# A w2 chunk loaded earlier, the fourfold copies and some ACT steps moved, and epsilon added on VectorE for two tiles

## The chip, the cores and the metric

One Trainium2 chip; the kernel runs on one of its cores. The metric is the device time of one execution in microseconds (us). Engines are called by their short names: PE is TensorE's matmul, PEld its weight load, DVE is VectorE, ACT is ScalarE, POOL is GpSimd, and SP is SyncE, which in this kernel issues nearly all DMA transfers.

## What is computed

The reference adds a residual, a linear attention and an MLP with squared ReLU, all on 2048 tokens of width 512:

```python
xn = _layernorm(x)                       # eps 1e-5
# A: 32 heads of 16
qkv = xn @ wqkv
phi = lambda t: where(t > 0, t + 1, exp(t)) + 1e-6
kv  = einsum("bhsd,bhse->bhde", phi(k), v)
z   = einsum("bhsd->bhd", phi(k))
o   = einsum("bhqd,bhde->bhqe", phi(q), kv) / (einsum("bhqd,bhd->bhq", phi(q), z) + 1e-6)
# B: F = 1376
h   = xn @ w1 + b1
h   = where(h > 0, h, 0) ** 2
return x + o @ wo + (h @ w2 + b2)
```

Inputs and output are float32. The kernel keeps that precision by splitting every operand into a high part in fp32r and the rest (a low part), and by running three matmuls (high by high, high by low, low by high) for each product.

## The kernel before, in words

The program is one long straight line for each engine: the order is written out by hand, and each engine runs its own instructions strictly in that order, waiting on semaphores. SP issues transfers in program order too, so a transfer that waits holds up those behind it.

**First part, tokens.** Sixteen tiles of 128 tokens are loaded, normalised (`measure` and `roots` for mean and root, `normalise`), transposed, projected onto k, and passed through phi. In `roots` (L239 to L243) POOL adds epsilon to the variance (L242) and raises it to the power -0.5 (L243); DVE then applies the result (L265). For each tile `kx` (L380 to L387) accumulates phi(k) against the tokens into four PSUM banks. Tokens carry a column of ones, so the last bank also holds the key sum z.

**Between the parts** (L864 to L985). The last `kx` is done, and ACT copies the four banks to `kxs` and one piece to `zrow` (L876). SP writes it to DRAM (`zd`, L878) and loads it back turned, in four transfers into `zc` (L882): these are the key sum's transfers. `zc` is first used well into the second part (L1125). PE forms the values and then, in `matrix`, four banks `pm`, which ACT copies (`matrix_copy`, tiles m); they are the attention matrix, needed split into mh and ml some 30 us later. The last chunk of w1 (96 of 128 columns, NF - 1 = 10) is applied ahead of the others as `pz` and `pz0b`, with ReLU into r2c. `piece_2(NF - 1, 0)` (L984) issues the loads of the last w2 chunk's rows (three transfers, L207, tile r2_10, shown as r) and returns two steps for later: `high` copies the rows on ACT into w2r (L210), sends part of that copy to another place of the same tile (L211) and, the first time only, makes the four copies w2q of 32 rows (L215); `low` has DVE compute the rest (L218, L219).

**Second part, two passes n = 0 and 1.** Each pass handles two blocks of 512 tokens, t1 and t2, with the transposed tokens x1 and x2. Pairs of weight chunks (two q chunks or two w1 chunks, `order`) are multiplied by both blocks with seven products instead of eight: sums S1 to S4 of weights (`chunk_sums`, split into `aop` by `chunk_split`) and sums T[1] to T[4] of tokens. Step p handles one pair; its PE order in step 0 of pass 0 is

- A by A11 with x1, then ACT copies bank A (c11, L1080);
- B by A12; then C by S1 with T[1], and ACT copies bank C (t5, L1097);
- `matrix` (pm, only here), then A by S2 with T[2], and ACT copies A (c12, L1162);
- C by S4 with x2, which needs the t5 copy to have read bank C;
- A by S3 with T[3], which needs the c12 copy to have read bank A;

and in step 1 the same again for the next pair, with the previous pair's last product (T[4], L1104, into the bank `before`) in between and, behind it, the first output product: `second_sums` (L1187) calls `last_2` (L493), eight matmuls on `acc` of the last w2 chunk with sz. sz is the squared r2c in fp32r, made by `last_units` (L960, ACT twice, then a transfer inside sz at L465 and DVE's rest in `rests`). Tiles T[3] and T[4] get their high parts on ACT and their low parts on DVE in `last_sums` (L1123, L1179); in the profile T_1014 is T[3] and T_1015 is T[4].

`next_2(t)` (L1002) carries out the two waiting steps of a w2 chunk (`high`, `low`) and issues the load of the next chunk. In the kernel before, `next_2(0)` stands at L1082, right behind the c11 copy of step 0. Raw weights of all kinds pass through one ring of six buffers (tag "raw"): a load waits until the last reader of the tile that held its buffer is done. `load_1` issues the two loads of a q or w1 pair (rq, r1) two steps ahead.

In the lines below a tile has no number, so r stands for r1, r2 and their like; the PSUM banks of the products are b, and c and t are the copies c11, c12 and t5.

Of the kernel before, what the change touches and what calls it, by code (L numbers as in the profile page):

```python
# [8 lines left out]
F32R = mybir.dt.float32r  # L9
AF = mybir.ActivationFunctionType  # L10
OP = mybir.AluOpType
# [7 lines left out]
def kernel(  # L19
# [30 lines left out]
    nc = tc.nc  # L50
# [9 lines left out]
    NF = -(-F // P)  # L60
# [11 lines left out]
    keep = ctx.enter_context(tc.tile_pool(name="keep", bufs=1))  # L72
# [5 lines left out]
    def bank(name, tag="ps"):  # L78
        return psum.tile([P, 512], F32, name=name, tag=tag)

    def w512(name, tag, bufs):
        return work.tile([P, 512], F32, name=name, tag=tag, bufs=bufs)
# [8 lines left out]
    def two(name):  # L91
        return keep.tile([P, 2, 512], F32, name=name, tag=next_tag("x"))

    def four(name, tag, dt=F32, pool=None):
        return (pool or work).tile([P, TB, 512], dt, name=name, tag=tag)
# [4 lines left out]
    def f32(ap):  # L100
        return ap.bitcast(F32)
# [7 lines left out]
    def copy(eng, o, i, bias=0.0):  # L109
        if eng == "act":  # L110
            nc.scalar.activation(o, i, AF.Copy, bias=bias)  # L111
        elif bias:
            ENG[eng].tensor_scalar(o, i, bias, None, op0=OP.add)
        else:
            ENG[eng].tensor_copy(o, i)
# [5 lines left out]
    def rest_of(l, src, h):  # L121
        nc.vector.tensor_tensor(out=l, in0=src, in1=f32(h), op=OP.subtract)  # L122
# [40 lines left out]
    def raw(name, src):  # L163
        t = w512(name, "raw", 6)
        nc.sync.dma_start(t[:, :src.shape[-1]], src)
        return t
# [6 lines left out]
    def units(f):  # L173


        if f < NF - 1:
            return [(0, f * P, P)]
        return [(0, f * P + Q, 2 * Q), (2 * Q, f * P, Q), (3 * Q, f * P, Q)]
# [5 lines left out]
            nc.sync.dma_start(tj[:, :, a:a + n], w1[:, o:o + n].rearrange("(j p) n -> p j n", j=NJ))  # L184
        return t

    w2r = []

    def load_o():
        o = wos[0] = four("wo", "ra")  # L190
# [6 lines left out]
    def piece_2(f, at):  # L197

        h, l = w2s[f] = [w2r[at // 2][:, at % 2 * 2 + u] for u in range(2)]
        if f < NF - 1:  # L200
            t = raw(f"r2_{f}", w2[f * P:(f + 1) * P, :])
            return [lambda: copy("act", h, t), lambda: rest_of(l, t, h)]


        t = w512(f"r2_{f}", "raw", 6)
        for a, o, n in units(f):
            nc.sync.dma_start(t[a:a + n], w2[o:o + n, :])  # L207

        def high():
            copy("act", h, t)  # L210
            nc.sync.dma_start(f32(l[2 * Q:]), f32(h[:2 * Q]))  # L211
            if "q" not in w2s:
                w2s["q"] = work.tile([P, D], F32R, name="w2q", tag="w2q")
                for k in range(TB):
                    nc.sync.dma_start(f32(w2s["q"][k * Q:(k + 1) * Q]), f32(h[2 * Q:3 * Q]))  # L215

        def low():
            rest_of(l[:2 * Q], t[:2 * Q], h[:2 * Q])  # L218
            rest_of(h[3 * Q:], t[3 * Q:], h[3 * Q:])  # L219

        return [high, low]
# [17 lines left out]
    def roots(tiles, st, mv, y):  # L239

        n = len(tiles)
        nc.gpsimd.tensor_scalar(y[:, 1, :n], mv[:, :n, 1], 1e-5, None, op0=OP.add)  # L242
        nc.gpsimd.tensor_tensor(out=y[:, 0, :n], in0=y[:, 1, :n], in1=power[:, :n], op=OP.pow)  # L243

    def normalise(tiles, st, mv, y):
# [206 lines left out]
    def quarters(name, r, h, pool, tag):  # L452

        lq = pool.tile([P, P], F32R, name=f"{name}q", tag=tag)
        for k in range(TB):
            at, to = slice(2 * Q, 3 * Q), slice(k * P, (k + 1) * P)
            rest_of(lq[k * Q:(k + 1) * Q], r[at, to], h[at, to])
        return lq

    def hidden_last(name, r):  # L460

        s = pair(name)
        h, hl = s[:, 0], s[:, 1]
        copy("act", h, r)
        nc.sync.dma_start(f32(hl[:2 * Q]), f32(h[:2 * Q]))  # L465

        def rests():
            rest_of(hl[2 * Q:], r[:2 * Q], h[:2 * Q])

        return (h, hl), rests  # L470

    def relu(o, i, f):
        nc.scalar.activation(o, i, AF.Relu, bias=b1s[:, f:f + 1])

    def plain_1(ps, w, x):

        for j in range(NJ):
            three(ps, [w[:, u, j * P:(j + 1) * P] for u in range(2)],
                  [x[u][:, j, :] for u in range(2)], j == 0, j == NJ - 1)
# [63 lines left out]
    for i0 in range(0, NT, TB):  # L543
# [5 lines left out]
        n = TB if i0 >= NPE else TB // 2  # L549
# [105 lines left out]
    def tokens_sum(n, tag):  # L655
        return keep.tile([P, 2, 2, 512], F32R, name=f"T{n}", tag=tag)
# [51 lines left out]
    def load_1(kind, n):  # L708
        load = raw_1 if kind == "w" else raw_q
        return [load(2 * n + k).rearrange("p (c n) -> p c n", c=2) for k in range(2)]  # L710
# [25 lines left out]
    def do(what, k=1):  # L736
        for _ in range(k):
            if what:
                what.pop(0)()
# [41 lines left out]
    def more(i=None):  # L781

        if i is None or i > 12:
            do(extra, counts[0].pop(0))
# [77 lines left out]
        more(i)  # L862

    T.update({n: tokens_sum(n, f"A{n - 3}") for n in (3, 4)})  # L864
    xlast = [xsb[(b + 1) % 2] for b in (NB - 1, NB - 2)]
    more()
    pz = bank("pz0")
# [47 lines left out]
    def matrix_copy(j, ps):  # L915
        if j % 2 == 0:
            mraw.append(two(f"m{j}"))
        copy("act", mraw[j // 2][:, j % 2], ps[j])
# [5 lines left out]


    last = TB - 1
    w2r = [four(f"w2r{k}", f"C{k}", F32R, keep) for k in range(2)]
    for n in range(2):
        t1, t2 = NB - 1 - 2 * n, NB - 2 - 2 * n
        x1, x2 = xsb  # L930
# [29 lines left out]
        def last_units(rz):  # L960
            nc.scalar.activation(rz, rz, AF.Square)
            sz, rests = hidden_last(f"sz{n}", rz)

            def packed():
                lqs.append(quarters(f"sz{n}", rz, sz[0], work, "heads"))

            return sz, rests, packed
# [3 lines left out]
        if n == 0:  # L971

            more()
            pz2 = bank("pz0b")
            plain_1(pz2, z, x2)
            more()

            rz = r2[1]
            relu(rz, pz, NF - 1)
            relu(r2[NF - 1], pz2, NF - 1)  # L980
            do(extra, 2)
            values()
            do(extra, len(extra))
            w2next = piece_2(NF - 1, 0)  # L984
        else:  # L985
            w2next = []
            pz = bank(f"pz{n}", "acc")
            plain_1(pz, z, x1)
# [4 lines left out]
        if n:  # L993
            rz = w512(f"rz{n}", "p", 6)
            relu(rz, pz, NF - 1)
            sz, sz_rests, packed = last_units(rz)
# [5 lines left out]
        def next_2(t):  # L1002

            do(w2next, 2 - highs.pop(0))
            if t + 1 < NF and (n == 0 or t >= TB - 1):
                f = w2order[t + 1]
                w2next.extend(piece_2(f, place(f)))
# [40 lines left out]
        def step(k=1):  # L1048

            for _ in range(k):  # L1050
                do(steps[t1] or steps[t2])

        for p in range(NO + 1):
            at_p = AT[p]
            kind, k = order[p] if p < NO else ("", 0)
            fa, fb = 2 * k, 2 * k + 1

            was, k = order[p - 1] if p else ("", 0)
            pa, pb = 2 * k, 2 * k + 1
            A, before, B, C = banks[p % 2], banks[(p + 1) % 2], *banks[2:]  # L1060
# [17 lines left out]
            if kind:  # L1078
                c11 = w512(f"c11_{n}_{p}", "p", 6)
                copy("act", c11, A)  # L1080
                if n == 0 and p == 0:
                    next_2(0)  # L1082
                product(B, A12, [x[:, 2:] for x in x1], True, True)
                if kind == "w":
                    high_2()
                nc.vector.tensor_tensor(out=c11 if kind == "w" else q[t1][:, fa], in0=B, in1=c11, op=OP.add)
                if kind == "w":
                    relu(c11, c11, fa)
                else:
                    steps[t1] += steps_of(t1, fa, parts=True)  # L1090
                step(at_p[0])
# [25 lines left out]
            if p == 0:  # L1117
                def last_sums(k, *what):
                    for f in what:
                        for j in range(2):  # L1120
                            f(k, j, o34[k - 3][:, j])

                last_sums(3, difference_high, difference_low)  # L1123
            if p == 1:
                nc.vector.tensor_scalar(zc[:, 1], zc[:, 0], 1e-6, None, op0=OP.mult)  # L1125
                acc = [bank(f"acc{t1}_{k}", "acc") for k in range(TB)]
# [6 lines left out]
            elif not was:  # L1133

                if n == 0:
                    pm = matrix()
# [17 lines left out]
                s12, s34 = chunk_sums(p + 1, w)  # L1154
            if p + 2 < NO:
                w = load_1(*order[p + 2])
            step(at_p[3])
            if p == NO - 1 and n:
                do(bias, 2)
# [10 lines left out]
                chunk_split(0, 1, s12)  # L1170
            step(at_p[4])
            if n == 0 and p == 0:
                matrix_copy(2, pm)
            product(C, S4, [x[:, 2:] for x in x2], False, True)
            nc.vector.tensor_tensor(out=c12 if kind == "w" else q[t2][:, fa], in0=C, in1=c12, op=OP.add)
            if kind == "w":
# [21 lines left out]
                second_sums()  # L1198
            step(at_p[6])
            if n == 0 and p == 0:  # L1200
                matrix_copy(3, pm)
                sz, sz_rests, packed = last_units(rz)
            product(A, S3, [T[3][:, u] for u in range(2)])
            if p == NO - 3 + 1 - n:
                load_res(t1)
# [26 lines left out]
        f = NF - 2  # L1232
# [36 lines left out]
        for e, f in enumerate(waiting[:-2]):  # L1269
# [14 lines left out]
            if n == 0 and 1 <= e < 5:  # L1284
                k, u = divmod(e - 1, 2)
# [68 lines left out]
```

## Time and profile before

| what | us |
|---|---|
| median of 3 runs (lowest, highest) | 413.15 (412.41, 414.46) |
| the profiled execution, its own time | 413.63 |
| its span on the core | 411.9 |
| PE busy | 404.0 (98%) |
| PEld busy | 331.2 (80%) |
| DVE busy | 302.2 (73%) |
| ACT busy | 263.1 (64%) |
| POOL busy | 49.7 (12%) |

The profile is one execution. Times in it count from the span's start; some 1.7 us of the execution's own time lie outside the span. Matmuls are pipelined: a matmul of 512 columns is shown as some 0.39 us, while the next one starts 0.23 us after it. The granted clock of TensorE is full in all 40 slices of the span. The page's chain of waits, followed back from the end, runs 89% of the span on PE; it leaves PE between 97 and 122 us and in the first 17.

### The profile page before, as it was taken

To read this page: it belongs to the slowest core of one execution; us is meant where nothing else is said; L and a number is where in the kernel's file an instruction comes from. 1 tells how busy PE (TensorE), PEld (TensorE's weight loads), DVE (VectorE), ACT (ScalarE), POOL (GpSimd) and SP (SyncE) were. 2 spreads that over 40 slices of the span, in tenths; PEclk is the share of its full clock that TensorE was granted. 3 is DMA by queue.
4 is the path that set the end of the run, shared out by engine and by line. 5 is a ranking of instruction groups with operands and counts; after the bars stand their busy time and mean duration, and the time that the engine had idled before them with its cause. 6 is when DMAs were issued, how large, how long until landed. Compare 5 with 4: busy or idle time off the path is not lost.

```text
span 411.9 us, 5624 instructions
## 1 busy us (share of the span) xinstructions
PE 404.0 (98%) x1947; PEld 331.2 (80%) x1947; DVE 302.2 (73%) x550; ACT 263.1 (64%) x460; POOL 49.7 (12%) x83
## 2 busy tenths in 40 slices
PE   7999999999989999999999999999999999999996
PEld 6788888888678888888878888888888888878885
DVE  5885666587699898988449967567989686449833
ACT  4666667556687779788638631577587857737520
POOL 5442333220000000030000200000000200000200
PEclk9999999999999999999999999999999999999999
DMA  6949676800442221273357992411121881024612
GB/s 207 347 142 340 193 306 205 256 1 0 104 134 72 78 75 54 77 203 53 136 221 246 362 235 90 128 53 51 51 78 29 235 183 40 2 101 154 103 26 102
DMA packets 46462, 56.34 MB, mean 137 GB/s; under 512 B 8225, under 2 KB 29985, under 8 KB 45154
## 3 DMA queue, kind: packets, MB, share of 16 engines
q1 hardware_dynamic: 44130, 51.80, 38.9%
q0 software_dynamic: 2304, 4.20, 6.2%
q8 instruction: 15, 0.25, 0.2%
q14 instruction: 13, 0.11, 0.1%
HBM read 41.43 MB, written 13.37 MB: 133 GB/s over the span
## 4 chain that ended last, share of the span: by engine, by line
PE 89%; DMA 3%; ACT 2%; DVE 2%; issue 1%; SPq 1%; POOL 0%; ACTq 0%
PE acc L130 37%; PE b L485 29%; PE kx L386 10%; PE pk L366 9%; PE acc L496 2%; DMA x<-in_A_x_dram 1%; PE pz L130 1%; DMA r<-in_B_w_dram 1%; PE b L130 1%; DMA sz<-sz 1%; ACT T L111 0%; SPq L522 0%; ACT aop L111 0%; ACT kxs L111 0%; DVE aop L119 0%
## 5 line engine op out<-in xcount | busy, mean ns | idle before, releaser
L130 PE MATMUL acc<-w2r,s 128*128 128x512 f32 x477 | 112.8, 390 | 0.0
L130 PEld LDWEIGHTS acc<-w2r,s 128*128 128x128 f32 x477 | 89.4, 188 | 19.2 <-issue 0.7
L485 PE MATMUL b<-T,aop 128*128 128x512 f32 x336 | 83.6, 390 | 1.4 <-ACT c L111 1.4
L485 PEld LDWEIGHTS b<-T,aop 128*128 128x128 f32 x336 | 62.9, 188 | 15.6 <-ACT c L111 1.8
L1034 POOL DMA_DIRECT2D res<-in_B_b_dram x16 | 14.4, 1114 | 280.2 <-DVE S L718 88.7
L386 PE MATMUL kx<-pk,tok 128*128 128x512 f32 x192 | 46.6, 391 | 0.1
L386 PEld LDWEIGHTS kx<-pk,tok 128*128 128x128 f32 x192 | 35.8, 188 | 7.9 <-ACT pk L111 0.5
L485 PE MATMUL b<-xs0h,aop 128*128 128x512 f32 x112 | 36.9, 390 | 0.0
L130 PE MATMUL acc<-mh,aTsr 128*128 128x512 f32 x112 | 35.6, 389 | 0.0
L1042 DVE TENSOR_TENSOR res<-acc,res 128x512 f32<-128x512 f32 x16 | 11.0, 692 | 21.9 <-PE acc L130 19.1
L122 DVE TENSOR_TENSOR w2r<-r,w2r 128x512 fp32r<-128x512 f32 (+2 forms) x35 | 23.8, 683 | 3.6 <-ACT w2r L111 3.5
L119 POOL TENSOR_TENSOR tok<-xp,tok 128x512 fp32r<-128x512 f32 x16 | 21.1, 1320 | 43.2 <-ACT tok L111 43.2
L130 PEld LDWEIGHTS acc<-mh,aTsr 128*128 128x128 f32 x112 | 21.0, 188 | 4.4
L485 PEld LDWEIGHTS b<-xs0h,aop 128*128 128x128 f32 x112 | 21.0, 188 | 4.4
L111 ACT ACTIVATE aop<-S 128x512 fp32r<-128x512 f32 x28 | 17.5, 626 | 10.0 <-DVE S L718 10.0
L111 ACT ACTIVATE w2r<-r 128x512 fp32r<-128x512 f32 x32 | 19.7, 620 | 6.5 <-DMA r<-in_B_w_dram 4.4
L119 DVE TENSOR_TENSOR aop<-S,aop 128x512 fp32r<-128x512 f32 x28 | 19.3, 688 | 4.8 <-ACT aop L111 4.4
L119 DVE TENSOR_TENSOR s<-c,s 128x512 fp32r<-128x512 f32 x20 | 13.5, 689 | 11.5 <-ACT s L111 11.5
L485 PE MATMUL b<-xs0l,aop 128*128 128x512 f32 x56 | 21.8, 389 | 0.0
L130 PE MATMUL acc<-ml,aTsr 128*128 128x512 f32 x56 | 21.8, 389 | 0.0
L485 PE MATMUL b<-xs1h,aop 128*128 128x512 f32 x56 | 19.6, 391 | 0.4 <-ACT t L111 0.4
L111 ACT ACTIVATE T<-Tf 128x512 fp32r<-128x512 f32 x16 | 9.5, 625 | 16.1 <-DVE Tf L661 15.9
(188 smaller groups left out, 740.9 us busy)
## 6 DMA issues: line engine op xcount, KB each, us to landing
r<-in_B_w_dram SPq DMA_DIRECT2D x49, 256.0 KB, 3.1
res<-in_A_x_dram SPq DMA_DIRECT2D x8, 512.0 KB, 4.3
res<-in_B_b_dram POOLq DMA_DIRECT2D x16, 256.0 KB, 6.0
out_dram<-res SPq DMA_DIRECT2D x15, 256.0 KB, 2.1
via<-xp SPq DMA_DIRECT2D x5, 512.0 KB, 3.0
xg<-via SPq DMA_DIRECT2D x20, 128.0 KB, 2.6
xTd<-t SPq DMA_DIRECT2D x8, 256.0 KB, 4.2
x<-in_A_x_dram SPq DMA_DIRECT2D x4, 512.0 KB, 6.1
```

The source lines that it names most:

```text
L111: nc.scalar.activation(o, i, AF.Copy, bias=bias)
L119: ENG[el].tensor_tensor(out=l, in0=src, in1=f32(h), op=OP.subtract)
L122: nc.vector.tensor_tensor(out=l, in0=src, in1=f32(h), op=OP.subtract)
L130: nc.tensor.matmul(ps, lhsT=a[u], rhs=b[v], start=first and n == 0, stop=last and n == 2)
L366: nc.tensor.matmul(ps, lhsT=cols(i)[u][:, j, slot(i)], rhs=w[v][:, j, :], start=first and n == 0, stop=last and n == len(steps) - 1)
L386: nc.tensor.matmul(kxp[c], lhsT=tok[i][:, u, c * P:(c + 1) * P], rhs=pk[i][:, v], start=i == 0 and (u, v) == first, stop=i == NT - 1 and ( ...
L485: nc.tensor.matmul(ps, lhsT=a[u][:, j * P:(j + 1) * P], rhs=b[v][:, j, :], start=first and j == 0 and n == 0, stop=last and j == 1 and n == 2,
L496: nc.tensor.matmul(ps, lhsT=s[u][:, k * P:(k + 1) * P], rhs=w2s[NF - 1][u][:, a:z], start=first and u == 0, stop=stop and u == 1)
L1034: nc.gpsimd.dma_start(r[:, i], b2[None, :].partition_broadcast(P), accum_op=OP.add)
L1042: nc.vector.tensor_tensor(out=r[:, a:z], in0=ps, in1=r[:, a:z], op=OP.add)
```

## The change

Four edits. The load of the last w2 chunk (`piece_2`, and the tiles w2r with it) is issued ahead of the key sum's transfers. The steps on that chunk (`next_2(0)`) stand behind the t5 copy and the T[3] splits of step 0 instead of in front of the t5 copy, and the fourfold copies w2q are put off to step 1, behind its weight loads. In step 0 the third `matrix_copy` goes behind the T[4] splits, next to the fourth, and `last_units` (r2c squared, sz) goes ahead of the S4 product. In `roots` DVE adds epsilon for tiles 0 and 1, POOL for all others. Each engine executes the same instructions as before, but for the two that go from POOL to DVE; PE's order is unchanged.

```diff
-    w2r = []
+    w2r, fourfold = [], []
...
             if "q" not in w2s:
                 w2s["q"] = work.tile([P, D], F32R, name="w2q", tag="w2q")
+                fourfold.append(lambda: four_times(h))
+
+        def four_times(h):
                 for k in range(TB):
                     nc.sync.dma_start(f32(w2s["q"][k * Q:(k + 1) * Q]), f32(h[2 * Q:3 * Q]))
...
-        nc.gpsimd.tensor_scalar(y[:, 1, :n], mv[:, :n, 1], 1e-5, None, op0=OP.add)
+        (nc.vector if tiles[0] < 2 else nc.gpsimd).tensor_scalar(y[:, 1, :n], mv[:, :n, 1], 1e-5, None, op0=OP.add)
...
     T.update({n: tokens_sum(n, f"A{n - 3}") for n in (3, 4)})
+    w2r.extend(four(f"w2r{k}", f"C{k}", F32R, keep) for k in range(2))
+    w2next = piece_2(NF - 1, 0)
...
-    w2r = [four(f"w2r{k}", f"C{k}", F32R, keep) for k in range(2)]
...
-            w2next = piece_2(NF - 1, 0)
...
                 copy("act", c11, A)
-                if n == 0 and p == 0:
-                    next_2(0)
                 product(B, A12, [x[:, 2:] for x in x1], True, True)
...
                 last_sums(3, difference_high, difference_low)
+                if n == 0:
+                    next_2(0)
...
                 w = load_1(*order[p + 2])
+            if p == 1:
+                do(fourfold)
...
             if n == 0 and p == 0:
-                matrix_copy(2, pm)
+                sz, sz_rests, packed = last_units(rz)
             product(C, S4, [x[:, 2:] for x in x2], False, True)
...
             if n == 0 and p == 0:
+                matrix_copy(2, pm)
                 matrix_copy(3, pm)
-                sz, sz_rests, packed = last_units(rz)
```

## The prediction

> **What bounds the kernel now.** I read the table by stages first, then the order of time inside the one stage that has holes. Columns of the stages: length, then busy time of PE, PEld, DVE, ACT and POOL with instruction counts, the granted TensorE clock, the DMA share and GB/s.
>
> ```profile
> 16.83:98.40 81.57, 81.57 (x363) 67.54 (x364) 57.51 (x101) 50.98 (x87) 26.31 (x41) 1.00 0.59 197
> 98.40:123.58 25.18, 23.15 (x247) 17.26 (x247) 19.21 (x38) 19.46 (x37) 0.00 (x0) 1.00 0.37 97
> 123.58:411.90 288.32, 284.80 (x1269) 234.75 (x1268) 214.56 (x390) 184.26 (x320) 14.39 (x16) 1.00 0.40 116
> ```
>
> TensorE is full from 16.83 to 98.40, and from 123.58 nearly to the end (what is missing there lies behind the last matmul). The change touches no matmul, so time can only come out of the stage from 98.40 to 123.58, or out of the first 16.83 us. The matmuls of that stage (start, length, and in brackets the idle time before and who ended it):
>
> ```profile
> 106.56 1.52 PE L485 MATMUL b<-T,aop 128*128 128x512 f32 x6
> ...
> 109.08 1.65 PE L485 MATMUL b<-T,aop 128*128 128x512 f32 x6
> 111.10 0.50 PE L485 MATMUL b<-xs1h,aop 128*128 128x512 f32 x1 [0.37 <-ACT t L111]
> ...
> 114.12 1.64 PE L485 MATMUL b<-T,aop 128*128 128x512 f32 x6 [1.36 <-ACT c L111]
> ...
> 118.32 2.88 PE L485 MATMUL b<-T,aop 128*128 128x512 f32 x12
> 121.04 0.39 PE L496 MATMUL acc<-w2r,sz 128*128 128x512 f32 x1
> 121.73 1.85 PE L496 MATMUL acc<-w2r,sz 128*128 128x512 f32 x7 [0.30 <-DMA sz<-sz]
> ```
>
> Matmuls start every 0.227 us (118.32 to 121.04 is 2.72 for twelve); a busy span ends later because the last one drains, so I count lost time from starts. Six from 109.08 would be through at 110.44, and the row is 0.13 longer than the one at 106.56, so 110.57; six more (1.36) then reach 111.93, but the S3 product starts at 114.12: 2.19 lost on ACT's copies t and c. The second matmul on acc could start at 121.27 and starts at 121.73: 0.46 lost on the transfer of sz. That is 2.65 in all. Both copies are late for one reason, on ACT and SP:
>
> ```profile
> 102.30 2.61 SPq L882 DMA_DIRECT2D zc<-zd  x4
> 105.01 1.57 SPq L207 DMA_DIRECT2D r<-in_B_w_dram  x3
> 106.62 2.58 SPq L184 DMA_DIRECT2D r<-in_B_w_dram  x2
> ...
> 109.93 0.63 ACT L111 ACTIVATE w2r<-r 128x512 fp32r<-128x512 f32 x1 [3.87 <-DMA r<-in_B_w_dram]
> 110.47 0.58 ACT L111 ACTIVATE t<-b 128x512 f32<-128x512 f32 x1
> 110.95 1.14 ACT L111 ACTIVATE T<-Tf 128x512 fp32r<-128x512 f32 x2
> ...
> 112.94 0.64 ACT L111 ACTIVATE aop<-r 128x512 fp32r<-128x512 f32 x1
> 113.46 0.60 ACT L111 ACTIVATE c<-b 128x512 f32<-128x512 f32 x1
> ```
>
> The w2 rows are loaded behind the key sum's four transfers, ACT stands 3.87 us in front of w2r<-r, and t, T, m, aop and c queue behind it.
>
> **The change part by part: the early load.** Its buffer is the one whose last reader is VectorE's split of w1's last chunk:
>
> ```profile
> 88.08 0.68 DVE L119 TENSOR_TENSOR w1z<-r,w1z 128x512 fp32r<-128x512 f32 x1
> ...
> DMA to landing us min/median/max: 1.9/3.1/15.9
> ```
>
> SP has nothing else to issue between its loads before this and zd, so the three transfers go out from about 88.8 (1.57 to issue). Even with the longest landing in the trace they are there by 88.8 + 1.57 + 15.9 = 106.3. ACT now asks for them after t and T. Taking them out of SP's queue brings r_0 and r_1 (the row at 106.62) forward by 1.61, to 105.01.
>
> **ACT's new order** is c, t, T, T, w2r, m, m, aop, c. The S1 product ends at 106.56 + 1.52 = 108.08; with 0.05 for the hand-over (t ends 111.05, PE starts 111.10) t runs at 108.13 to 108.71. From t to aop are 112.94 - 110.47 = 2.47, plus the pitch of the inserted w2r, 110.47 - 109.93 = 0.54: aop at 111.14, c 0.52 later at 111.66, done at 112.26, and PE's S3 product starts at 112.32. TensorE is free at 111.93, so 0.39 of the wait stays. Against 114.12 this is **1.80 us**.
>
> Does aop find r_0? Before, it ran at 112.94 without a wait, so r_0 took at most 6.32 from its issue; at worst it lands at 111.33, 0.19 late. The median of 3.1 puts it at 108.1, and I take 0. The same shift holds for r_1 at its first reader, so its bound is 0.19 too.
>
> **VectorE and the reordered second half of the step.** Now T_1015 (T[4]) stands behind r2c and sz on ACT, so I follow it:
>
> ```profile
> 110.60 1.41 DVE L122 TENSOR_TENSOR w2r<-r,w2r 64x512 fp32r<-64x512 f32 x2 [3.52 <-ACT w2r L111]
> ...
> 113.84 0.69 DVE L119 TENSOR_TENSOR aop<-r,aop 128x512 fp32r<-128x512 f32 x1
> 114.90 0.43 DVE L718 TENSOR_TENSOR S<-S,r 128x256 f32<-128x256 f32 x1
> ...
> 115.42 0.63 ACT L111 ACTIVATE aop<-S 128x512 fp32r<-128x512 f32 x1 [1.05 <-DVE S L718]
> ...
> 117.45 1.29 DVE L122 TENSOR_TENSOR T<-Tf,T 128x512 fp32r<-128x512 f32 x2
> 117.96 0.63 ACT L961 ACTIVATE r2c<-r2c 128x512 f32<-128x512 f32 x1
> 118.62 0.64 ACT L111 ACTIVATE sz<-r2c 128x512 fp32r<-128x512 f32 x1
> 118.65 0.69 DVE L1066 TENSOR_TENSOR q<-b,t 128x512 f32<-128x512 f32 x1
> ...
> 119.33 2.26 DMA sz<-sz
> ```
>
> T's high halves end at 109.75, VectorE's low halves let w2r's low halves begin at 110.45, and these (0.72 each) let aop's begin at 111.89; before it was 113.84, so this chain is 1.95 earlier. ACT's aop<-S goes from 115.42 to 113.47, r2c follows at 114.01 (+0.54), sz at 114.67 (+0.66), T_1015 at 115.21, its halves done by 116.35. VectorE does the second low half at 116.4, and q (L1066) 0.60 later, at 117.07 to 117.76. TensorE needs T_1015 and a read-out bank after four products, 24 x 0.227 behind 112.32, at 117.76, and with the slow first matmul (0.12) at 117.88. So the step fits by some 0.1; before it fitted by 0.34. Each microsecond that this chain slips further is a microsecond of TensorE.
>
> sz is ready at 115.31, its transfer goes out at 115.38 and lands 2.26 later at 117.64; the matmul that waited for it now comes at 117.88 + 1.36 = 119.24. That wait, **0.46 us**, goes. The m copies of banks 2 and 3, moved behind, end near 117.2, before acc needs the banks.
>
> **The fourfold copies** leave SP's queue at 111.18 and come back behind r_3:
>
> ```profile
> 111.18 2.49 SPq L215 DMA_DIRECT2D w2q<-w2r  x4
> ...
> 122.00 16.44 SPq L184 DMA_DIRECT2D r<-in_B_w_dram  x4
> ...
> 148.32 0.62 ACT L111 ACTIVATE aop<-r 128x512 fp32r<-128x512 f32 x1
> ```
>
> The four loads from 122.00 (r_2 to r_5) take 16.44 because they wait for buffers; the last goes out near 138.1 and its pair is first read at 148.32. So 2.49 of issue lies under ten microseconds of slack: 0. Without that cover r_4 would be 2.49 late, and TensorE with it.
>
> **Epsilon on VectorE**, two 128x1 instructions:
>
> ```profile
> 4.54 0.24 POOL L242 TENSOR_SCALAR y<-mv 128x1 f32<-128x1 f32 x1 [1.39 <-DVE mv L232]
> 4.86 0.58 POOL L243 TENSOR_TENSOR y<-y,power 128x1 f32<-128x1 f32 x1
> 5.47 0.55 DVE L265 TENSOR_SCALAR xp<-x,mv,y 128x512 f32<-128x512 f32 x1 [0.32 <-POOL y L243]
> 6.54 0.43 DVE L115 CAST wkh<-rk 128x512 fp32r<-128x512 f32 x1 [0.52 <-DMA rk<-in_A_wqkv_dram]
> 10.14 0.56 POOL L242 TENSOR_SCALAR y<-mv 128x1 f32<-128x1 f32 x1 [1.40 <-DVE mv L232]
> 122.50 0.16 DVE L1125 TENSOR_SCALAR zc<-zc 128x4 f32<-128x4 f32 x1
> ```
>
> They cost VectorE 0.16 each by the nearest row, 0.32 together, which is the idle time before xp at 5.47; the first pow may start 0.1 earlier. What TensorE needs next is wkh, and that waits for the transfer of rk, to 6.54. So 0, between a loss of 0.2 (both instructions ahead of xp and nothing saved) and a gain of 0.4 (POOL's 0.24 and its hand-over, if rk were early). The Trainium skill, "SBUF — State Buffer", section "SBUF: two separate sides", says that a VectorE instruction with two SBUF inputs locks out a GpSimd instruction that reads SBUF for its whole length. By that rule the move would save the difference between 0.56 and 0.24, but the 0.56 stands at 10.14, for tile 2, which stays on POOL; tile 0 shows 0.24, so nothing is saved.
>
> **The sum:** 1.80 + 0.46 = 2.26. The profiled execution took 413.63 (span 411.9): 411.4. The median of the runs shown is 413.15, 0.48 lower, so I forecast **410.9**. Bounds: 2.65 if no wait is left (410.5); 1.88 if r_0 and r_1 are both at their worst (411.3).
>
> **The rivals.** First, the sz transfer collides. It used to start three microseconds after the loads rq; now it goes out at 115.4, just behind rq_3 (the last S moves 1.95 forward, so about 114.1).
>
> ```profile
> rq<-in_A_wqkv_dram SPq DMA_DIRECT2D x8, 256.0 KB, 4.6
> ```
>
> If sz needs 4.6 instead of 2.26, it lands at 119.98, 0.74 after its matmul's turn, and the gain is 1.52: 411.6. For it: the two transfers share the same 16 engines in the same microseconds. Against it: sz is a copy of its own tile that took 2.26, and it has 1.6 in hand. Second, the start gains as well (0.4): 410.5. For it, xp does wait for POOL; against it, rk. Third, the change doesn't do what it says: the early load finds its buffer taken until zd has gone, ACT still waits, 413.15. Against it is the reader at 88.08. Fourth, slower: r_1 lands late. On its landing wait aop's last split, S, and behind them on ACT now r2c, sz and T_1015 as well. It decides from 112.5 on (S), one for one; at 112.5 + 2.26 the gain is gone, at 116.9 the time is 415.2. That is 9 to 11 us after its issue; the trace has landings up to 15.9, but a median of 3.1, and the load now has fewer transfers ahead of it.
>
> **How the numbers follow.** Forecast 0.66, collision 0.11, start too 0.10, no effect 0.04, slower 0.09. A measurement of this kernel tells about 0.5% from no change, 2.07 us, so faster means under 411.1. The forecast's 410.9 lies just under it: I give 0.53 of its 0.66 to faster and 0.13 to the same. With the start 0.63 faster; with collision and no effect 0.28 the same; 0.09 slower. The range runs from 409.9 (410.5 less 0.6, since the runs shown spread by a microsecond to either side) to 412.5 (the collision's 411.6 with somewhat more); it leaves out no effect, slower and the far ends.
>
> **What would show it.** Right: no wait of ACT for a DMA before w2r; the S4 product directly behind S2; S3 some 0.4 late behind c; no wait for sz; from there to the end every matmul 2.3 earlier. Wrong: idle time of TensorE before the product with T_1015 (released by VectorE's q or ACT's T), a wait for sz, a wait for r in ACT's aop, or a wait for r_4 near 148. A first key-sum matmul off 16.83 by over 0.2 would refute the zero at the start.

## The result and the profile after

| what | before | after |
|---|---|---|
| median (lowest, highest) of 18 runs each, us | 413.16 (411.22, 414.79) | 411.97 (410.83, 412.73) |
| ratio, 95% interval | | 0.9973 (0.9960 to 0.9985) |
| the profiled execution, its own time, us | 413.63 | 411.82 |
| its span on the core, us | 411.9 | 410.1 |
| PE busy, us | 404.0 (98%) | 404.5 (99%) |

The change makes the kernel 1.2 us faster. 2.26 was forecast; the time lies within the range.

Read the two profiled executions by stages first. The next fence is the table of stages of the kernel after, the one behind it that of the kernel before (stretch, length, then busy time of PE, PEld, DVE, ACT and POOL, clock, DMA share, GB/s). The cuts are starts of matmuls that both kernels have: the first matmul of the key sum (kx), the first into pz0b, the first on b behind the eight of `last_2`, the first `acc<-w2r,s` at the end of pass 0's blocks, and the first on b of pass 1.

```profile
16.40:99.07 82.67, 82.67 (x370) 68.43 (x369) 59.40 (x103) 52.04 (x90) 26.21 (x41) 1.00 0.60 199
99.07:120.67 21.60, 21.39 (x242) 16.20 (x240) 17.39 (x33) 17.52 (x34) 0.00 (x0) 1.00 0.34 87
120.67:248.09 127.42, 127.42 (x567) 104.96 (x566) 104.07 (x191) 89.72 (x157) 7.31 (x8) 1.00 0.51 149
248.09:256.28 8.19, 7.56 (x34) 5.93 (x32) 5.41 (x10) 1.42 (x3) 0.00 (x0) 1.00 0.37 130
256.28:410.10 153.82, 150.31 (x672) 123.92 (x670) 105.55 (x193) 93.55 (x162) 7.07 (x8) 1.00 0.34 88
```

```profile
16.83:99.57 82.74, 82.74 (x368) 68.48 (x369) 58.64 (x103) 52.14 (x90) 26.31 (x41) 1.00 0.58 194
99.57:123.42 23.85, 21.82 (x242) 16.16 (x240) 17.93 (x35) 18.14 (x35) 0.00 (x0) 1.00 0.39 102
123.42:250.82 127.40, 127.40 (x567) 104.96 (x566) 105.10 (x192) 90.69 (x158) 7.31 (x8) 1.00 0.49 147
250.82:258.08 7.26, 7.26 (x34) 6.01 (x32) 4.00 (x7) 0.00 (x0) 0.00 (x0) 1.00 0.41 148
258.08:411.90 153.82, 150.30 (x672) 123.94 (x670) 105.61 (x193) 93.73 (x162) 7.08 (x8) 1.00 0.33 88
```

The stage of the change is 2.25 shorter (23.85 to 21.60), as forecast (2.26). But the stretch from 248.09, which took 7.26, takes 8.19: 0.93 is given back there. The first 16 us are 0.43 shorter and the stretch behind them 0.07; the rest is equal. 0.43 + 0.07 + 2.25 - 0.02 - 0.93 = 1.80, the difference of the spans.

Inside the stage the steps stand where the prediction put them. The timelines of SP, ACT, PE and DVE of the kernel after (start, length, and in brackets the idle time before and who ended it; the clock of this execution is 0.50 ahead, 99.07 for 99.57):

```profile
89.09 1.57 SPq L207 DMA_DIRECT2D r<-in_B_w_dram  x3
...
107.59 0.60 ACT L111 ACTIVATE t<-b 128x512 f32<-128x512 f32 x1 [2.06 <-PE b L488]
108.09 1.15 ACT L111 ACTIVATE T<-Tf 128x512 fp32r<-128x512 f32 x2
109.13 0.62 ACT L111 ACTIVATE w2r<-r 128x512 fp32r<-128x512 f32 x1
109.65 1.07 ACT L111 ACTIVATE m<-pm 128x512 f32<-128x512 f32 x2
110.61 0.64 ACT L111 ACTIVATE aop<-r 128x512 fp32r<-128x512 f32 x1
111.13 0.60 ACT L111 ACTIVATE c<-b 128x512 f32<-128x512 f32 x1
...
111.78 1.66 PE L488 MATMUL b<-T,aop 128*128 128x512 f32 x6 [0.21 <-ACT c L111]
...
115.33 1.29 DVE L122 TENSOR_TENSOR T<-Tf,T 128x512 fp32r<-128x512 f32 x2 [0.26 <-ACT T L111]
116.54 0.68 DVE L1069 TENSOR_TENSOR q<-b,t 128x512 f32<-128x512 f32 x1
...
118.83 2.00 PE L499 MATMUL acc<-w2r,sz 128*128 128x512 f32 x8
```

w2r has no bracket: ACT waits for no rows any more. S3 starts at 111.78, on the old clock 112.28 (forecast 112.32). The eight matmuls on acc run without a wait for sz. What is new is at 249. The view of PE's waits after has a row that the profiled execution of before lacks (engine, tile, line, releaser, us in total, times, longest):

```profile
PE acc L130 <- DVE s L119: 0.6, 1, 0.6
```

PE's timeline shows where it stands:

```profile
248.09 0.62 PE L130 MATMUL acc<-w2r,s 128*128 128x512 f32 x2
249.34 0.50 PE L130 MATMUL acc<-w2r,s 128*128 128x512 f32 x1 [0.63 <-DVE s L119]
```

The third matmul was due 2 x 0.227 behind 248.09, at 248.54, and comes at 249.34.

### The profile page after: what moved, and what is told of

It reads as the page before. It is cut to its first block, busy times and chain, and to the rows that moved or that the text cites. A ratio compares the mean times of both kernels' runs of the same rounds, so it can differ in the third digit from the quotient of the medians.

```text
span 410.1 us, 5621 instructions
## 1 busy us (share of the span) xinstructions
PE 404.5 (99%) x1947; PEld 332.3 (81%) x1947; DVE 303.2 (74%) x552; ACT 262.7 (64%) x460; POOL 48.7 (12%) x81
## 4 chain that ended last, share of the span: by engine, by line
PE 85%; DMA 6%; DVE 4%; ACT 2%; SPq 1%; issue 1%; ACTq 0%
PE b L488 31%; PE acc L130 28%; PE pk L369 11%; PE kx L389 10%; DMA r<-in_B_w_dram 5%; PE acc L499 2%; PE pz L130 1%; PE b L130 1%; DVE s L119 1%; DMA x<-in_A_x_dram 1%; PE pt L308 1%; SPq L207 0%; ACT aop L111 0%; ACT kxs L111 0%; ACT T L111 0%
## 5 line engine op out<-in xcount | busy, mean ns | idle before, releaser
L488 PE MATMUL b<-xs0l,aop 128*128 128x512 f32 x56 | 21.8, 389 | 0.0
L130 PE MATMUL acc<-ml,aTsr 128*128 128x512 f32 x56 | 21.8, 389 | 0.0
L111 ACT ACTIVATE T<-Tf 128x512 fp32r<-128x512 f32 x16 | 9.5, 624 | 16.1 <-DVE Tf L664 15.9
```

Source lines behind the costliest of these rows:

```text
L130: nc.tensor.matmul(ps, lhsT=a[u], rhs=b[v], start=first and n == 0, stop=last and n == 2)
L488: nc.tensor.matmul(ps, lhsT=a[u][:, j * P:(j + 1) * P], rhs=b[v][:, j, :], start=first and j == 0 and n == 0, stop=last and j == 1 and n == 2,
```

## What stands at 249

Towards the end of pass 0, step e = 7 of the loop over w2 chunks calls `zs()`: it splits w1's last chunk for pass 1 into w1z, on ACT and then on DVE. The program has this split ahead of the splits of s, which TensorE needs for the last matmuls on acc. The timelines of ACT, DVE and PE there, in the kernel before:

```profile
243.83 0.64 ACT L111 ACTIVATE w1z<-r 128x512 fp32r<-128x512 f32 x1 [2.57 <-DMA r<-in_B_w_dram]
...
249.82 0.68 DVE L119 TENSOR_TENSOR s<-r2c,s 128x512 fp32r<-128x512 f32 x1
...
250.82 0.85 PE L130 MATMUL acc<-w2r,s 128*128 128x512 f32 x3
```

And in the kernel after:

```profile
242.62 0.63 ACT L111 ACTIVATE w1z<-r 128x512 fp32r<-128x512 f32 x1 [4.11 <-DMA r<-in_B_w_dram]
...
248.61 0.68 DVE L119 TENSOR_TENSOR s<-r2c,s 128x512 fp32r<-128x512 f32 x1
```

Its chain of waits has the load in front of that w1z (start, length, what), and its stages show the transfers:

```profile
225.48 17.04 DMA r<-in_B_w_dram
```

```profile
231.00:237.00 6.00, 6.00 (x29) 4.95 (x28) 5.97 (x10) 1.45 (x3) 0.88 (x1) 1.00 1.05 317
237.00:243.00 6.00, 6.00 (x28) 4.98 (x27) 1.50 (x3) 1.64 (x3) 0.00 (x0) 1.00 1.10 224
```

Before, s was done at 249.82 + 0.68 = 250.50 and its matmul due at 250.82 + 0.45 = 251.27: 0.73 in hand, allowing 0.04 for the hand-over. After, TensorE comes 2.73 earlier. The split comes only 1.21 earlier, since it waits for a load that takes 17.04 (8.46 of these SP spends on issuing it); the DMA engines are full meanwhile (shares of 1.05 and 1.10), with the reloaded tokens of pass 1 above all, which were issued ahead of it. 2.73 - 1.21 - 0.73 = 0.79 is lost, as the row at 249.34 shows (0.80).

## The experiments

Lengths below are of two stretches, each read from one profiled execution per run: the **stage** (first matmul into pz0b to first on b behind `last_2`) and the **group** (first `acc<-w2r,s` behind 248 to the next on b; 7.26 if nothing waits). Where nothing else is said the run is of 6 to 12 times, beside the kernel before on the same chip.

### The wait at 249: a_zs and b_zs

The split moves behind the last two splits of s; a_zs is the changed kernel with it, b_zs the kernel before with it.

```diff
-                if e == 7:
-                    zs()
...
             if k < 2:
                 wait_for(last_two[1 - k])
+            if n == 0 and k == 1:
+                zs()
```

> The changed kernel with one step moved: the split of w1's last chunk for pass 1 (w1z, ACT then VectorE) comes after the last two hidden chunks are split (s<-r2c) and not in front of them. Theory A, the gain is given back because ACT stands in front of w1z for a transfer of the DMA-bound stretch (225 to 243 us) and PE's last-two products wait 0.9 us behind it: the wait at 249 shrinks to 0.3 or less and the time falls by 0.6 to 0.9 us, to about 411.2. Theory B, the loads land when the DMA engines let them and the next load (rq) binds at the same place: no change (within 0.2). Theory C, the 0.9 us is chance of one execution: no change in the median.

Measured: 410.95 (410.81 to 412.16), ratio 0.9956 (0.9942 to 0.9970); stage 21.58, group 7.26. In its timeline s no longer stands behind w1z:

```profile
246.59 0.69 DVE L119 TENSOR_TENSOR s<-r2c,s 128x512 fp32r<-128x512 f32 x1
247.19 0.68 DVE L119 TENSOR_TENSOR w1z<-r,w1z 128x512 fp32r<-128x512 f32 x1
...
248.09 0.85 PE L130 MATMUL acc<-w2r,s 128*128 128x512 f32 x3
```

> The kernel before with the same step moved. Theory A: the kernel before had 0.3 to 0.6 us in hand at this place in its profile, so at most executions with late loads gain; 0 to 0.3 us faster, 412.9 to 413.2. Theory B: no change. If it gains as much as the changed kernel does, the wait was there already and didn't take the gain back.

Measured: 411.27 (410.99 to 413.36), ratio 0.9969 (0.9952 to 0.9987). So the wait at 249 costs the kernel after about 1.0. The expectation for b_zs (412.9 to 413.2) missed: the kernel before was at 413.04 beside it, so the same move gains 1.77 by the medians there, and 0.54 to 1.98 by the interval of the ratio. That is no less than the kernel after gains, so by the expectation's own last sentence the wait was there before the change already, though the profile of before shows nothing. The times of b_zs fall into two groups: eight from 410.99 to 411.55, three from 412.58 to 413.36; the profiled one is the longest, with a stage of 23.85. Two microseconds between executions of one kernel, and one of them of the length on which the forecast was built: that led to the second question.

### Epsilon alone: a_noeps and b_eps

a_noeps is the changed kernel with epsilon on POOL for all tiles, b_eps the kernel before with DVE adding it for tiles 0 and 1 (the line of `roots` in the diff).

> The changed kernel with epsilon on POOL for all tiles, as before. My forecast put this part at 0: no change (within 0.2 us), the start's 0.43 us in the profile being chance. Rival: the start did gain by it, then this is 0.3 to 0.5 slower than the changed kernel, and PE's first key-sum matmul is back at 16.8.

Measured: 411.89 (410.82 to 412.74), ratio 0.9973 (0.9955 to 0.9990), to the digit that of the change.

> The kernel before with only epsilon on VectorE for tiles 0 and 1. Forecast: 0 (within 0.2 us). Rival: 0.3 to 0.5 us faster than the kernel before, first key-sum matmul at 16.4.

Measured: 413.40 (411.15 to 415.40), ratio 1.0010 (0.9989 to 1.0031). No gain from epsilon is seen; the medians alone, with these intervals, could hide some tenths. The first key-sum matmul stands at 16.39 in a_noeps and 16.51 in b_eps, at 16.40 and 16.62 in two profiles of the kernel after, at 16.83, 16.33 and 16.51 in profiles of the kernel before. Over all profiles of this document it stands at 16.52 on average with epsilon on VectorE (eight, 16.32 to 16.77) and at 16.59 without (ten, 16.33 to 16.95): the 0.43 of the first pair is chance.

But the profile of b_eps, whose stage is that of the kernel before, shows it 21.93 long and not 23.85.

### How long the stage is in other executions: b_look, b_look2, b_look3, a_look

Unchanged kernels, profiled again; the table takes in the pair above, b_eps and a_noeps, since no effect of epsilon is seen.

> The kernel before, unchanged, profiled a second time. Theory (varying landing): the four zc transfers issue in either 1.75 or 2.6 to 2.9 us and the w2 rows land 1.9 or 3.6 us behind their issue; with the first the stage is 21.9 long, with the second 23.85. Rival (the kernel before always shows 23.85, and the other length belongs to epsilon on VectorE): 23.85 with zc at 2.6 or more.

> The kernel before, unchanged, profiled a third time, to see how often the rows come late. Theory: stage 21.9 to 22.1 or 23.85, and TensorE's group behind 248 is 7.3 long with the second and 7.8 to 8.0 with the first. Rival (a third length): something else lies between.

> The kernel before, unchanged, a fourth profile: as the third.

> The changed kernel, unchanged, profiled a second time. Theory (with the load at 89 nothing in this stage depends on a late landing): stage 21.6, group behind 248 8.2 to 8.4 long unless something ahead made TensorE late by as much. Rival: a stage of 22 or more.

| execution | stage | group | own time |
|---|---|---|---|
| before | 23.85 | 7.26 | 413.63 |
| b_look | 22.06 | 8.01 | 413.47 |
| b_look2 | 23.20 | 8.45 | 413.72 |
| b_look3 | 22.09 | 8.25 | 412.48 |
| b_eps | 21.93 | 7.78 | 411.84 |
| mean of these five | 22.63 | 7.95 | 413.03 |
| after | 21.60 | 8.19 | 411.82 |
| a_look | 21.59 | 7.97 | 411.95 |
| a_noeps | 21.58 | 8.32 | 411.94 |
| mean of these three | 21.59 | 8.16 | 411.90 |

The rival of b_look falls: the kernel before, unchanged, has the short stage too. So does the expected pairing of a long stage with a short group: b_look2 has both long. After the change the stage is the same to 0.02. The profile of b_zs, whose edit lies behind the stage, is a sixth with the stage of before: with its 23.85 the mean is 22.83. The group of before is 0.69 longer on average than the 7.26 of b_zs; a gain of 0.69 lies within that run's interval (0.54 to 1.98). Where the short and the long stage differ is seen in SP's issues and ACT's wait. First the rows of these source lines in before, b_look2 and b_look3 (shortest/median/longest ns of one issue, first and last start):

```profile
L882 SPq DMA_DIRECT2D zc<-zd x4: 332/425/1284, 102.3 to 103.6; - x4
L207 SPq DMA_DIRECT2D r<-in_B_w_dram x3: 419/482/582, 105.0 to 106.2; - x3
```

```profile
L882 SPq DMA_DIRECT2D zc<-zd x4: 333/423/1314, 101.8 to 103.1; - x4
L207 SPq DMA_DIRECT2D r<-in_B_w_dram x3: 419/482/582, 104.6 to 105.7; - x3
```

```profile
L882 SPq DMA_DIRECT2D zc<-zd x4: 332/422/437, 101.9 to 103.2; - x4
L207 SPq DMA_DIRECT2D r<-in_B_w_dram x3: 419/582/1318, 103.7 to 105.7; - x3
```

Then ACT's timeline in b_look2 and in b_look3:

```profile
108.85 0.63 ACT L111 ACTIVATE w2r<-r 128x512 fp32r<-128x512 f32 x1 [3.29 <-DMA r<-in_B_w_dram]
```

```profile
107.80 0.63 ACT L111 ACTIVATE w2r<-r 128x512 fp32r<-128x512 f32 x1 [2.17 <-DMA r<-in_B_w_dram]
```

One of the seven issues takes 1.3 us (1.5 in b_zs) instead of 0.3 to 0.6. Where it is one of zc, ACT waits 3.3 to 3.9 for the rows; where it is one of the rows' own, 2.0 to 2.2. The S3 product then misses its turn by 0.3 at most instead of 1.4.

But the slow issue doesn't send the last rows later. In all six executions the last of the three transfers goes out 3.8 to 4.1 behind the first of zc; what differs is how long it takes to land, 3.12 to 3.75 in the first kind and 1.88 to 2.04 in the second. The chain of waits shows it, of the kernel before and of b_look3:

```profile
106.16 3.75 DMA r<-in_B_w_dram
```

```profile
105.73 2.04 DMA r<-in_B_w_dram
```

The two issues behind the rows are slower in the first kind as well (1.89 to 2.58 together, against 0.97). What makes both slow, no run tells.

b_look has in addition a wait long before the change, behind a late transfer of turned tokens (PE's timeline); it makes the stretch up to pz0b 84.09 long instead of 82.7:

```profile
51.24 0.50 PE L366 MATMUL pk<-wkh,xs1h 128*128 128x512 f32 x1 [1.05 <-ACT xs1h L321]
```

### The parts alone: b_early, b_late, b_swap

b_early is the kernel before with nothing but the load (and the w2r tiles) ahead of the key sum; b_late with nothing but `next_2(0)` behind the T[3] splits. b_swap leaves the load at its time and puts the four zc loads behind it:

```diff
-    for k in range(NJ):
-        nc.sync.dma_start(zc[32 * k:32 * (k + 1), 0], of_g[k])
...
             w2next = piece_2(NF - 1, 0)
+            for k in range(NJ):
+                nc.sync.dma_start(zc[32 * k:32 * (k + 1), 0], of_g[k])
```

> The kernel before, with the other part alone: the load of the w2 rows and the w2r tiles stand ahead of the key sum's transfers; next_2(0), sz, the fourfold copies and the m copies stay where they were. Theory (varying landing): ACT never waits for the rows, w2r runs at about 106.1 in front of t, the stage is 21.8 to 22.2 long in every execution, and the time is that of the changed kernel plus up to the 0.46 of sz: 411.8 to 412.4. Rival (the order counts, not the load): w2r and its steps on VectorE in front of t and T hold these up by 0.6 to 1.2, stage 22.5 or more, median 412.6 or more.

Measured: 411.54 (410.57 to 414.43), ratio 0.9965 (0.9943 to 0.9987); stage 21.27, group 8.36. The load alone does all that the change does, and its stage is 0.3 shorter: w2r runs in ACT's idle time ahead of t, c is done earlier and S3 waits for nothing. The expectation for the stage, 21.8 to 22.2, had kept the late c and the full 0.46 of sz in it.

> The kernel before, with one part of the change alone: next_2(0) stands behind the t5 copy and the T[3] splits; the load of the w2 rows stays behind the key sum's transfers, sz and the m copies stay where they were. Theory (the landing of the key sum's transfers and of the rows behind them varies between executions by some 2 us, and the order of ACT's steps alone takes that out of the path): ACT asks for the rows at about 109.1, they land between 107.6 and 109.9, so S3 loses 0 to 0.8 us; the stage from pz0b to the first matmul on b behind last_2 is 21.9 to 22.7 long in every execution (before 23.85 in one, 21.93 in another), and the median is near that of the changed kernel, 411.5 to 412.2. Rival (it is the early load that brings the gain, the order alone nothing): stage 23.85 where the rows land late, median 413.0.

Measured: 412.06 (411.07 to 413.47), ratio 0.9973 (0.9954 to 0.9993); stage 21.88, ACT asks for the rows at 111.01 and finds them. The order alone reaches the change's ratio as well. This profile is of the kind whose rows land early (the slow issue, 1.38, is one of the rows' own), where the kernel before has 21.93 to 22.09 anyway; that the order covers late rows too rests on the ratio. By the ratios either part alone gains as much as the whole change; together they don't add.

> The kernel before, with the four loads of the turned key sum (zc) issued behind the load of the last w2 chunk's rows instead of in front of it; the rows still go out at about 101, after zd, and all steps stay where they were. Theory (in some executions the zc loads issue and land late, and the rows late behind them): the rows are there by 106, ACT does not wait for them, the stage from pz0b to the first matmul on b behind last_2 is 21.2 to 21.9 long as with the load at 89, and the median is that of the early load alone, 411.5, within 0.4. Rival (the rows land late in some executions by themselves, whatever is ahead of them): ACT waits 2 or 4 for them in front of w2r, the stage is 21.9 or 23.9, the median 412.8 or more.

Measured: 411.76 (410.34 to 413.42), ratio 0.9960 (0.9940 to 0.9979); stage 21.25. The slow issue is there again and again falls on zc, but the rows are ahead of it (SP's timeline and ACT's):

```profile
101.58 1.58 SPq L207 DMA_DIRECT2D r<-in_B_w_dram  x3
103.20 3.02 SPq L984 DMA_DIRECT2D zc<-zd  x4
...
105.90 0.62 ACT L111 ACTIVATE w2r<-r 128x512 fp32r<-128x512 f32 x1
```

So the rows were late for their place behind the key sum's transfers, and an exchange of two neighbours cures it: they go out 3.4 earlier than in the kernel before (101.58 for 105.01) and land no faster, 2.4 to 3.4 behind their issues (2.1 to 3.7 before). The Trainium skill, "DMA: Bandwidth & Descriptors", section "Queues, rings and completion order", says that each DMA engine takes the descriptors of one issuing queue in their order. The run fits that (nothing but the order changed, and the wait of 2 to 3.9 is gone), but does not show it, since SP itself sends the rows that much earlier.

### The term for sz: a_sz and c_sz

`matrix_copy(2)` and `last_units` go back to their places of before, in the changed kernel (a_sz) and in a_zs (c_sz).

> The changed kernel, with matrix_copy(2) and last_units put back to their places of before, so that sz is made behind the T[4] splits again. Theory (what is won here is given back at 249, where TensorE waits for w1's split behind the loads): the wait of last_2 for sz returns with 0.2 to 0.5 us, the stage is 21.8 to 22.1 long, the wait at 249 shrinks by as much, and the time stays within 0.2 of the changed kernel's: 411.9 to 412.2. Rival (each term of the sum counts in full): the time is 0.46 longer, 412.4, with the wait at 249 as long as before. Second rival (sz has room): no wait for sz, the stage 21.6 and the time unchanged.

Measured: 412.17 (410.91 to 413.00), ratio 0.9981 (0.9963 to 1.0000); stage 21.85, group 8.44. The stage lengthens as expected, but the group did not shrink by it in this execution; 0.2 in the median lies within the intervals.

> a_zs with matrix_copy(2) and last_units put back to their places of before. In the changed kernel this cost 0.25 in the stage and 0.2 in the median. Theory: with the wait at 249 gone the stage is again 21.85 long and the whole difference reaches the end: 0.25 more than a_zs, 411.1 to 411.4. Rival (sz's 0.46 counts in full): 0.46 more. Second rival: no difference.

Measured: 411.24 (410.99 to 411.64), ratio 0.9948 (0.9929 to 0.9967); stage 21.85 against 21.58, and 0.29 in the median, though the two ran on two chips and by their ratios c_sz is not the slower one (0.9948 against 0.9956, inside both intervals). In the two profiles, where nothing waits at 249, the 0.27 of the stage reaches the end: it is still there at the end of the group (255.79 against 255.35, of which 0.16 stood there ahead of the stage). From the first matmul on acc to the next on b are 2.21 in c_sz and 1.81 in a_zs, 0.40 for the wait; 0.13 of it is paid ahead, where T_1015 now comes late on ACT and, behind its split, VectorE's q, which reads out the bank that its product needs (q ends at 117.27 in a_zs, at 117.08 in c_sz; the product spans 3.00 and 2.88).

### A better version: c_next, b_both, c_b1

c_next is a_zs with `next_2(0)` back behind the c11 copy. b_both is the kernel before with the early load and the moved split alone. c_b1 is c_next with the loads of b1 behind the token pieces xg in SP's queue, against the wait at 51.

> a_zs (the changed kernel with the split of w1's chunk for pass 1 moved), with next_2(0) put back right behind the c11 copy; the early load, the late fourfold copies and the early sz stay. Theory (with the rows landed in time, the place of next_2 is of small account, and the old one is a little better because w2r then runs in ACT's idle time in front of t): c for S3 is ready 0.4 to 0.5 earlier, no wait of TensorE there, the stage from pz0b to the first matmul on b behind last_2 is 21.1 to 21.4 long (a_zs: 21.58), no wait at 249, median 410.5 to 410.9. Rival (the new place is part of the gain): w2r and its rests on VectorE delay T_1014 or T_1015, the stage is 21.8 or more, median 411.2 or more.

> The kernel before with two moves alone: the load of the last w2 chunk ahead of the key sum, and the split of w1's chunk for pass 1 behind the output matmuls that it held up. Theory (these two places hold all that is to be had; the new places of next_2, sz and the fourfold copies bring nothing more): stage 21.3 as in the run with the early load alone, no wait at 249, median 410.7 to 411.1, not above a_zs. Rival (the rest of the change counts): 0.4 or more above a_zs, 411.4 or more.

> c_next, with the four loads of b1 behind the pieces of xg of the same token tile in SP's queue instead of in front of them. In two of ten profiles TensorE stands some 1.0 in front of the transposed tokens xs1h at about 51, because xg is issued at 43 and lands 6.6 later instead of 4.3. Theory: xg goes out 3 to 5 earlier, this wait is in no execution, the median is that of c_next or up to 0.4 below it, and the spread of the times is smaller (all within 1.0 of the lowest). Rival (a later transfer, via or the next xg, is late instead): TensorE waits behind 52, median above c_next.

| kernel | median (lowest, highest) | ratio, 95% interval | stage | group |
|---|---|---|---|---|
| c_next | 410.43 (409.94, 410.75) | 0.9939 (0.9916 to 0.9961) | 20.99 | 7.26 |
| b_both | 410.57 (410.23, 410.88) | 0.9943 (0.9920 to 0.9966) | 21.27 | 7.25 |
| c_b1 | 410.35 (410.21, 410.53) | 0.9938 (0.9914 to 0.9962) | 20.98 | 7.26 |

All three beat the kernel before, and their medians are 1.4 to 1.6 below that of the change, which did not run beside them. c_next and b_both came out somewhat better than expected (a stage of 20.99 for 21.1 to 21.4, medians of 410.43 and 410.57 for 410.5 and 410.7 at the best). b_both shows that two moves carry nearly all of it. c_next's stage has no idle time left:

```profile
99.47:120.46 20.99, 20.99 (x241) 16.27 (x240) 17.49 (x33) 17.53 (x34) 0.00 (x0) 1.00 0.33 90
```

c_b1 can't be told from c_next. Its xg went out at 42.87, 0.9 earlier than c_next's and not 3 to 5, since xg itself waits for `via` (issued at 36.50, landed 6.3 later). None of the 30 times of c_next, b_both, c_b1 and c_sz lies over 0.5 above its median, so the wait at 51 did not show in them, with or without the move.

## Why the prediction was right and wrong

**Right: the steps inside the stage.** On the old clock t came at 108.09 (forecast 108.13), aop at 111.11 (111.14) without a wait for r_0, S3 at 112.28 (112.32), r2c at 114.00 (114.01), q at 117.04 (117.07). The wait for sz went. The fourfold copies went out at 124.99 of the new clock, and ACT's aop<-r, at 148.32 before, ran there at 145.58 without a wait. Epsilon gave nothing that is seen; the check named for it (first key-sum matmul within 0.2 of 16.83) was a bad one, since it moves by 0.5 without any change.

**Wrong: the size of the sum, 1.80 + 0.46 = 2.26.** The steps are right for the execution that it was read from: the stage came out 2.25 shorter. But it was read from one execution, and that had the longest stage of the five of the kernel before. The prediction saw that its execution was 0.48 above the median and only subtracted this from the time; it did not ask which of the waits it was removing made the execution slow. Over five executions the stage was 22.63 long on average and after the change 21.59: the stage gains 1.04, not 2.26 (1.24 with b_zs as a sixth). With rows that come early it gains 0.33 to 0.50. Of the two terms, 1.80 is the one that varies with the rows. The 0.46 for sz was put too high as well: undoing that part costs the stage 0.25 in a_sz and 0.27 in c_sz, since the wait is 0.40 there and the product with T_1015, which the sum had fitting by 0.1, loses 0.13.

**Wrong: "from there to the end every matmul 2.3 earlier".** The step behind it was the reading that TensorE is full from 123.58 nearly to the end. A full TensorE shows that nothing was late by then, not how much was in hand. At 249 it was 0.73, and the profile of before, with no wait there, hid that other executions of the same kernel do wait: in four of the five the group was 7.78 to 8.45 long. On average the group went from 7.95 to 8.16, another 0.21 lost; the 0.93 of the first pair is mostly that its execution of before did not wait there.

**What is left.** 1.04 - 0.21 = 0.83 by these executions, whose own times differ by 1.13 on average (413.03 to 411.90); the medians of 18 runs each differ by 1.19. Most of the rest is the wait at 51 in one of the five executions of before (1.4, or 0.28 on average); it stands in the profile of b_late too (0.88). Of the four edits only epsilon acts ahead of it, and the runs with epsilon alone show no difference; whether it comes less often after the change, eight executions can't tell.

**Of the rivals**, none came true: sz did not collide with rq, the start did not gain, r_1 was not late. What took the gain's place, a wait that an earlier TensorE runs into 130 us further on, was not among them. What would have pointed to it was the stretch with the DMA engines full, from 225 to 243, and ACT's wait for w1's rows at its end (2.57 before). The longest landing in the trace, 15.9, which the prediction used as a bound for the early load, belongs to that very stretch (15.4 to 15.9 for the three loads issued from 227.2 to 228.3). That the time still fell into the range is luck: its upper end was set for a collision of sz that didn't happen.

## What to carry to other kernels

Before a stall from one profile becomes a term of a sum, profile the same kernel a few times: a wait that ends with a transfer can differ by two microseconds between executions, and the median pays its average, not the one that was seen. When TensorE is to come earlier, look along the whole span for the operand that is ready last before its use and count what is in hand, above all behind stretches in which the DMA engines are full; in-order engines pass one late load on to every instruction behind it. And a load whose buffer is free should go out ahead of small scattered transfers that nobody needs soon: here that single move brought as much as the whole change.

## What the runs showed of the hardware

- In six profiles of the kernel before (b_eps and b_zs among them, whose edits lie elsewhere), exactly one of SP's seven issues in a row (four zc, three r) took 1.28 to 1.51 us, the others 0.33 to 0.59. It fell on zc in three executions (stages 23.85, 23.85, 23.20) and on r in three (21.93, 22.06, 22.09). The last r went out 3.8 to 4.1 behind the first zc in both kinds, but took 3.12 to 3.75 to land in the first and 1.88 to 2.04 in the second. What makes the slow issue, what decides where it falls, and why the rows land later in the first kind, no run tells.
- A load of w1 whose like lands in a median of 3.0 us took 17.04 in a stretch whose DMA share was 1.0 to 1.1, and SP spent 8.46 of it on the issue. In the kernel before the loads at this place took 15.4 to 15.9.
- Two executions of one kernel can take nearly the same time for different reasons: 1.4 lost at 51 in b_look, 0.75 at 249 and a short stage gave 413.47; the execution with the long stage and neither wait took 413.63.
